# A fused DFT and SwiGLU kernel: three value units per tile seeded by ScalarE, one mirrored value kept in its bank, one row moved to another queue

## The chip, the cores and the metric

The kernel runs on one core of a Trainium2 chip. A core has five engines with their own instruction streams: TensorE (PE in the profile, with its weight loads as PEld), VectorE (DVE), ScalarE (ACT), GpSimd (POOL) and SyncE (SP). Each works through its stream in the order in which the program emits it, and they wait for each other through semaphores. Matrix products land in PSUM, which has eight banks here in use as three for gate values (g), three for values (v) and two for outputs (o).

The metric is the device time of one execution in microseconds. The median of three runs of the kernel before is 638.0 us (635.74 to 638.57).

## The reference

The input x has the shape (8, 3008, 256). It is transformed by a Fourier transform along both the sequence and the feature axis, and the real part of the result, as 24064 rows of 256, goes through a gated feed-forward block with 1536 inner features.

```python
X = np.fft.fft(x, axis=1); X = np.fft.fft(X, axis=2); x = X.real      # (24064, 256)
g = x @ w_gate
silu = g * (1.0 / (1.0 + np.exp(-g)))
val = x @ w_val
out = silu * val @ w_out
```

## The kernel before

The real part of a two-dimensional transform is symmetric: row k and row -k of a batch are a sum and a difference of the same two parts, an even part P and an odd part Q. So the kernel computes P and Q for half of the rows (12032 columns) and gets two output rows from each column. The columns are cut into 24 tiles: four widths of 512 and two of 480 in the first six (tiles 0 and 3 are 480 wide), then 512, and 320 plus 8 single columns in the last.

The feature transform is folded into the weights. Wp and Wq are the cosine and sine transforms of w_gate and w_val, and Wm is Wq times -2, with its first row (the one of frequency 0 and 128, which has its own sign) set to 0. So the direct value of a column is Wp P + Wq Q, and the mirrored value is the direct one plus Wm Q.

The main loop (line 954) runs over 288 **units** u = (t, f): tile t, and block f of 128 inner features, twelve per tile. For each unit `part_a` makes the direct gate and value, and `part_b`, one unit later, the mirrored ones. The products feed an output product with Wo (`OWork`, line 722), whose eight matmuls per unit are spread over the units of the next tile, and whose results ScalarE evicts to EV (line 709) before SP stores them.

There are two forms of unit.

- A **whole** unit has six matmuls: g gets Wp P and Wq Q, v gets Wp P and Wq Q, then after the direct values are read, Wm Q is added to g and to v. ScalarE takes Silu of g twice (L809 and L827), and DVE multiplies twice (L810 into hp, L828 into hm).
- A **split** unit has five. DVE forms es, the part of the value that the mirrored row shares, from the bank after Wp P alone and the first row of Q: es = bc * w0 + e (L795). `bc` is that row of Q copied to all partitions, and w0 the first row of the sine-transformed w_val. After Wq Q is added (in `odd`, emitted one unit later), DVE makes hp (L799), and the mirrored value as 2 es - e into an SBUF tile VV, in reversed order (L801). ScalarE writes Silu of the mirrored gate reversed (sgv, L823), and POOL, which works on SBUF alone, multiplies the two into hm (L824).

`WHOLE` (line 761) lists the whole units: all of tile 0, units 0 and 6 of tile 1, 2 and 9 of tile 2, 2 and 10 of tile 3, unit 10 of every later tile, and 10 and 11 of the last. That makes 39 whole units and 249 split ones.

The banks rotate (`Banks`, line 82): a unit takes the bank that has been unused longest, so that with three value banks unit f takes that of unit f-3. A transform (`transform`, line 594) takes one out of turn (aside).

Within one turn of the loop for unit i the order on each engine is the order of emission. First come the row steps and other work due before it, then `part_a(i)`: on PE g from Wp and Wq, then the value's Wp; on ScalarE sg; on DVE es. Then four output matmuls; then `odd` of unit i-1: on PE the value's Wq, on DVE hp and the mirrored value; then `part_b(i-1)`: on PE Wm into the gate, on ScalarE the mirrored Silu, and the product. Then an eviction, if one is due, four more output matmuls, folding steps on POOL, and a transform if one is due. Transforms are emitted after units 4 and 6 of tiles 2, 3, 5, 6, 7, 9, 10, 12, 13, 15, 16, 18, 19 and 21. They come in two parts: part 0 for the transforms of tiles 2, 5, 7, 10, 13, 16 and 19, part 1 for the others.

The row bc of tile t+1 goes by way of DRAM: `store_row0` (L944) ahead of unit 7 of tile t, `load_row0` (L949) ahead of unit 9, both by SP's queue, where the loads of x and the stores of the output stand too.

Of the kernel before, what the change touches and what calls it, by code (L numbers as in the profile page):

```python
# [12 lines left out]
F32 = mybir.dt.float32  # L13
I32 = mybir.dt.int32
BF16 = mybir.dt.bfloat16
AF = mybir.ActivationFunctionType
Alu = mybir.AluOpType
# [14 lines left out]
def kernel(  # L32
# [8 lines left out]
    nc = tc.nc  # L41
    B, M, D = x.shape
    Dff = moe_w_gate.shape[1]
    P = 128
# [4 lines left out]
    nF = Dff // P  # L49
    T = 512  # L50
# [6 lines left out]
    nT = len(wide)  # L57
# [4 lines left out]
    NOO = NCE + GH + 1  # L62
    NTAB = NOO + G
# [3 lines left out]
    def width(t):  # L67
        return wide[t]
# [5 lines left out]
    const = ctx.enter_context(tc.tile_pool(name="const", bufs=1))  # L74
# [7 lines left out]
    class Banks:  # L82
# [2 lines left out]

        def __init__(self, nm):
            self.line = [psB.tile([P, T], F32, name=f"{nm}{i}") for i in range(3)]

        def tile(self, shape=None, dt=None, name=None, aside=False):
            b = self.line.pop(0)  # L90
            self.line.insert(1 if aside else 2, b)
            return b if shape is None or len(shape) == 2 else b.rearrange("p (q d) -> p q d", q=shape[1])

    psG, psV = Banks("g"), Banks("v")

    Wp = const.tile([P, 2, Dff], BF16, name="Wp")
    Wq = const.tile([P, 2, Dff], BF16, name="Wq")
    Wm = const.tile([P, 2, Dff], BF16, name="Wm")
# [4 lines left out]
    w0 = const.tile([P, nF], F32, name="w0")  # L103
# [4 lines left out]
    mM = const.tile([P, 4], F32, name="mM")  # L108
    wC = const.tile([P, 1], F32, name="wC")
    sgn = const.tile([P, 1], F32, name="sgn")  # L110
    XA = const.tile([P, 8, 2, D], F32, name="XA")
    XC = const.tile([P, 8, 2, D], F32, name="XC")
    CEs = {(nm, i): const.tile([P, 2, 2, 3 * P + 1], BF16, name=f"CE{nm}{i}") for nm in "ac" for i in range(2)}
# [6 lines left out]
    VV = const.tile([P, 4, T], F32, name="VV")  # L120
# [7 lines left out]
    def next_of(big, what):  # L128
        turn[what] += 1
        return big[:, (turn[what] - 1) % 4]  # L130
# [138 lines left out]
    for hi in range(2):  # L269
        q.dma_start(out=XC3[64 * hi:64 * hi + NCR, 0:2, :],  # L270
                    in_=rows_at(0, 2 * (P + 1) - 1 + 2 * hi * R, [[2 * D, NCR], [R * D, 2], [1, 2 * D]]))
    for hi in range(2):
        for a in range(2):
            q.dma_start(out=XC3[64 * hi:64 * hi + NCR, 2 + a, :],
                        in_=down_set(0, 3 - 2 * hi - a, JC, LC, NC_))
    q.dma_start(out=XC0[NCR:64 + NCR + 1:64, 0:2, 1],
                in_=rows_at(0, 0, [[2 * R * D, 2], [R * D, 2], [1, D]]))
# [79 lines left out]
    def weigh(lo, hi):  # L357
        vts(Tab[:, 1, 1, :, lo:hi], Tab[:, 1, 1, :, lo:hi], scalar1=wC, scalar2=None, op0=Alu.mult)
# [120 lines left out]
    def value_rows(fcs):  # L479

        n = T // P
        ps = psO.tile([P, T], F32, name="o")
        for fc in fcs:
            src = W0[1] if fc == 0 else Wraw[1][:, :, (fc - 1) * T:fc * T]
            for f in range(n):
                for no in range(2):
                    nc.tensor.matmul(ps[:, fc * n + f:fc * n + f + 1], src[:, no, f * P:(f + 1) * P],
                                     SDt[:, no, 0:1], start=(no == 0), stop=(no == 1))
        nc.scalar.copy(w0[:, fcs[0] * n:(fcs[-1] + 1) * n], ps[:, fcs[0] * n:(fcs[-1] + 1) * n])
# [73 lines left out]
    def pq_tiles(t):  # L563
        if t not in ptile:
            w = width(t) + B if t == nT - 1 else T
            ptile[t] = (pqp if t < nT - 1 else const).tile([P, w], BF16, name="Pt")
            qtile[t] = (pqp if t < nT - 1 else const).tile([P, w], BF16, name="Qt")
        return ptile[t], qtile[t]
# [186 lines left out]
    units = [(t, f) for t in range(nT) for f in range(nF)]  # L755
# [2 lines left out]
    owork = None  # L758

    ROW0 = (7, 9)  # L760
    WHOLE = {0: range(nF), 1: (0, 6), 2: (2, 9), 3: (2, 10), nT - 1: (10, 11)}

    bc = {}

    def split(u):

        return u[1] not in WHOLE.get(u[0], (10,))

    def part_a(u):
        t, f = u  # L770
        n = width(t)
        w = n + (B if t == nT - 1 else 0)
        fs = slice(f * P, (f + 1) * P)
        if f == 0:
            hts[t] = (hp.tile([P, nF, T + B], BF16, name="hp"), hp.tile([P, nF, T], BF16, name="hm"))
        Pt, Qt = pq_tiles(t)

        def mm(ps, Wt, gv, src, start, stop):
            nc.tensor.matmul(ps[:, :w], Wt[:, gv, fs], src[:, :w], start=start, stop=stop,  # L779
                             skip_group_check=True)  # L780

        g = psG.tile([P, T], F32, name="g")
        mm(g, Wp, 0, Pt, True, False)
        if u == (0, 0):
            v = psV.tile([P, T], F32, name="v")
            mm(v, Wp, 1, Pt, True, False)
        mm(g, Wq, 0, Qt, False, True)
        if split(u):
            e = psV.tile([P, T], F32, name="v")
            mm(e, Wp, 1, Pt, True, False)  # L790
            sg = sgp.tile([P, T], F32, name="sg")
            nc.scalar.activation(sg[:, :w], g[:, :w], AF.Silu)  # L792
            stt = nc.vector.scalar_tensor_tensor
            es = esp.tile([P, T], F32, name="es")
            stt(es[:, :n], bc[t][:, :n], w0[:, f:f + 1], e[:, :n], op0=Alu.mult, op1=Alu.add)  # L795

            def odd():
                mm(e, Wq, 1, Qt, False, True)
                nc.vector.tensor_tensor(hts[t][0][:, f, :w], sg[:, :w], e[:, :w], op=Alu.mult)  # L799
                vm = next_of(VV, "vv")  # L800
                stt(vm[:, n - 1::-1], es[:, :n], 2.0, e[:, :n], op0=Alu.mult, op1=Alu.subtract)  # L801
                state[u] = (g, vm)
            return odd
        if u != (0, 0):
            v = psV.tile([P, T], F32, name="v")
            mm(v, Wp, 1, Pt, True, False)
        mm(v, Wq, 1, Qt, False, True)
        sg = sgp.tile([P, T], F32, name="sg")
        nc.scalar.activation(sg[:, :w], g[:, :w], AF.Silu)  # L809
        nc.vector.tensor_tensor(hts[t][0][:, f, :w], sg[:, :w], v[:, :w], op=Alu.mult)  # L810
        state[u] = (g, v)

    def part_b(u):
        t, f = u
        w = width(t)
        Pt, Qt = pq_tiles(t)
        g, v = state.pop(u)
        for gv, ps in ((0, g), (1, v))[:1 if split(u) else 2]:
            nc.tensor.matmul(ps[:, :w], Wm[:, gv, f * P:(f + 1) * P], Qt[:, :w], start=False, stop=True,  # L819
                             skip_group_check=True)  # L820
        if split(u):
            sg = sgv.tile([P, T], F32, name="sgv")
            nc.scalar.activation(sg[:, w - 1::-1], g[:, :w], AF.Silu)  # L823
            nc.gpsimd.tensor_tensor(hts[t][1][:, f, :w], sg[:, :w], v[:, :w], op=Alu.mult)  # L824
            return
        sg = sgp.tile([P, T], F32, name="sg")
        nc.scalar.activation(sg[:, :w], g[:, :w], AF.Silu)  # L827
        nc.vector.tensor_tensor(hts[t][1][:, f, w - 1::-1], sg[:, :w], v[:, :w], op=Alu.mult)  # L828
# [12 lines left out]
    for b in range(2, B, 2):  # L841
        u = slot[(b, 0)] - 1
# [64 lines left out]
    job_at = {}  # L907
    for jb in jobs[1:]:
        u = slot[jb]
# [13 lines left out]
    def sine_o(ch):  # L923
# [2 lines left out]
    late = angles_o(1)  # L926
    before = {0: late[0:1], 1: weight_unit(1, 0) + late[1:2], 2: weight_unit(1, 1) + cosine_o(0), 3: late[2:3],
              4: weight_unit(2, 0), 5: weight_unit(2, 1) + cosine_o(1), 7: sine_o(0), 8: sine_o(1),
              9: [lambda: weigh(NOO, NTAB), lambda: value_rows((1, 2))]}
    loads = []  # L930

    def spread_row0(t):
# [5 lines left out]

    row0d = {}

    def store_row0(t):
        w = width(t) + (B if t == nT - 1 else 0)
        row0d[t] = rdp.tile([1, T], BF16, name="row0")
        nc.sync.dma_start(out=row0d[t][:, :w], in_=pq_tiles(t)[1][0:1, :w])  # L944

    def load_row0(t):
        w = width(t) + (B if t == nT - 1 else 0)
        bc[t] = bcp.tile([P, T], BF16, name="bc")
        nc.sync.dma_start(out=bc[t][:, :w], in_=row0d.pop(t)[0, :w].partition_broadcast(P))  # L949

    prev = None
    odd = None
# [1 line left out]
    for i, u in enumerate(units):  # L954
        t, f = u
        if (t, f) == (1, 0):
            spread_row0(t)
        if 0 < t < nT - 1 and f in ROW0:
            (store_row0, load_row0)[ROW0.index(f)](t + 1)
        for fn in before.pop(i, ()):  # L960
            fn()
        run_loads(i)
        coming = part_a(u)
        if owork:
            owork.run(4)
        if odd:
            odd()
        odd = coming
        if prev is not None:
            part_b(prev)  # L970
            run_evicts()
            if prev[1] == nF - 1:
                owork = OWork(prev[0], hts[prev[0]])
                owork.run(4)
        if owork and not (prev is not None and prev[1] == nF - 1):
            owork.run(4)
        for what, j in fold_at.get(i, ()):
            fold_step(what, j, i)
        for what in act_at.pop(i, ()):
            load_next(what)  # L980
        if i in job_at:
            transform(*job_at[i])
        prev = u
# [38 lines left out]
```

## Time and profile before

| What | Value |
|---|---|
| median of 3 runs | 638.0 us |
| profiled execution, whole time | 638.3 us |
| its span, first to last instruction | 636.5 us |
| mean granted TensorE clock | 0.997 |
| DVE es (L795), 128x512 | 229 of 746 ns |
| DVE mirrored value (L801), 128x512 | 229 of 681 ns |
| POOL product (L824), 128x512 | 229 of 1278 ns |
| ScalarE Silu (L792), 128x512 | 229 of 602 ns |
| ScalarE eviction (L709), 128x512 | 90 of 580 ns |

A line of the profile's page of groups gives the source line, the engine and operation, what it writes and reads, the shape and count, then the busy time in us, the mean of one in ns, and the idle time ahead of it with what ended it. A line of the timeline gives the start in us from the beginning of the span, the duration in us, the engine, the source line, the operation and its tiles, and in brackets the idle time of the engine ahead of it with its releaser. PE's matmuls are pipelined: one of 512 columns has a duration of 0.38 us there, but the next starts 0.22 us later, and the chain of waits counts it so. A line of a table of windows gives the stretch, its length, then the busy time of PE, PEld, DVE, ACT and POOL with their counts, the granted clock of PE, the share of the DMA engines and their rate.

### The profile page before, as it was taken

The page shows a single profiled execution, that of the slowest core. Times are in us where ns is not written, and L with a number is a line of the kernel's source. Part 1 is how long each engine was busy: PE and PEld are TensorE (multiplying, and loading weights), DVE is VectorE, ACT ScalarE, POOL GpSimd, SP SyncE. Part 2 cuts the span into 40 slices and gives each one's busy share as a digit, 9 for nine tenths or more (in the row PEclk, how much of TensorE's full clock was granted, in tenths as well). Part 3 has the DMA queues.
Part 4 walks back from the last instruction along what each step waited for, and adds up shares of the span by engine and source line. Part 5 has one row for each costly group of instructions (what it writes and reads, how often), then busy time and mean ns, then how long its engine had stood idle before and what let it go on. Part 6 is the DMA issues. An engine that isn't in the chain of part 4 may idle for free.

```text
span 636.5 us, 13211 instructions
## 1 busy us (share of the span) xinstructions
PE 620.9 (98%) x4166; PEld 400.8 (63%) x4232; DVE 580.3 (91%) x1040; ACT 414.8 (65%) x744; POOL 516.9 (81%) x534
## 2 busy tenths in 40 slices
PE   8999998999999999999999999999999999999997
PEld 5446665666666666666666666656666666666686
DVE  7889996999999999999999999999999999999992
ACT  7686664666666666666666666666666666666663
POOL 9997998799699999996997988997798655655651
PEclk9999998999999999999999999999999999999999
DMA  9683224425322513245224511134211111111212
GB/s 228 117 170 82 82 83 147 126 74 147 100 70 79 165 44 86 66 93 147 76 78 105 131 43 52 45 84 140 58 47 47 42 51 44 58 46 46 57 50 76
DMA packets 52980, 55.41 MB, mean 87 GB/s; under 512 B 7504, under 2 KB 44238, under 8 KB 52910
## 3 DMA queue, kind: packets, MB, share of 16 engines
q1 hardware_dynamic: 49726, 52.20, 29.2%
q0 software_dynamic: 3184, 2.36, 2.5%
q8 instruction: 33, 0.54, 0.4%
q14 instruction: 37, 0.30, 0.2%
HBM read 32.22 MB, written 24.67 MB: 89 GB/s over the span
## 4 chain that ended last, share of the span: by engine, by line
PE 80%; DVE 11%; issue 2%; ACT 1%; DMA 1%; SPq 0%; POOL 0%; DVEq 0%; ACTq 0%
PE o L749 34%; PE v L779 19%; PE g L779 15%; PE g L819 8%; DVE hp L799 4%; DVE VV L801 2%; DVE Pt L639 2%; PE v L607 2%; DVE es L795 2%; PE v L819 1%; PE g L607 1%; DMA bc<-row 1%; PE o L466 0%; ACT sg L809 0%; DVE hp L810 0%
## 5 line engine op out<-in xcount | busy, mean ns | idle before, releaser
L824 POOL TENSOR_TENSOR hm<-sgv,VV 128x512 bf16<-128x512 f32 (+2 forms) x249 | 312.2, 1259 | 98.6 <-DVE VV L801 77.9
L823 ACT ACTIVATE sgv<-g 128x512 f32<-128x512 f32 (+2 forms) x249 | 146.9, 590 | 130.9 <-PE g L819 125.6
L795 DVE SCALAR_TENSOR_TENSOR es<-bc,w,v 128x512 f32<-128x512 bf16 (+2 forms) x249 | 183.4, 736 | 23.0 <-DMA bc<-row 4.3
L792 ACT ACTIVATE sg<-g 128x512 f32<-128x512 f32 (+2 forms) x249 | 148.0, 594 | 46.8 <-PE g L779 33.4
L749 PE MATMUL o<-Wo,hp 128*128 128x256 bf16 (+2 forms) x1140 | 170.5, 273 | 0.0
L749 PE MATMUL o<-Wo,hm 128*128 128x256 bf16 (+2 forms) x1140 | 169.6, 273 | 0.0
L799 DVE TENSOR_TENSOR hp<-sg,v 128x512 bf16<-128x512 f32 (+2 forms) x249 | 167.4, 672 | 0.3 <-PE v L779 0.2
L801 DVE SCALAR_TENSOR_TENSOR VV<-es,v 128x512 f32<-128x512 f32 (+2 forms) x249 | 167.3, 672 | 0.0
L749 PEld LDWEIGHTS <-hp 128*128 128x128 bf16 (+2 forms) x1140 | 112.5, 99 | 70.9 <-issue 2.4
L749 PEld LDWEIGHTS <-hm 128*128 128x128 bf16 (+2 forms) x1140 | 111.9, 98 | 71.4 <-issue 3.5
L779 PE MATMUL v<-Pt,Wp 128*128 128x512 bf16 (+2 forms) x288 | 108.1, 375 | 5.3 <-DVE VV L801 2.3
L779 PE MATMUL v<-Qt,Wq 128*128 128x512 bf16 (+2 forms) x288 | 108.2, 376 | 2.8 <-DVE es L795 2.8
L819 PE MATMUL g<-Qt,Wm 128*128 128x512 bf16 (+2 forms) x288 | 108.1, 375 | 0.7 <-ACT sg L809 0.7
L779 PE MATMUL g<-Pt,Wp 128*128 128x512 bf16 (+2 forms) x288 | 108.4, 377 | 0.1
L779 PE MATMUL g<-Qt,Wq 128*128 128x512 bf16 (+2 forms) x224 | 83.9, 375 | 0.3 <-DVE Qt L639 0.3
L779 PEld LDWEIGHTS <-Wp 128*128 128x128 bf16 x576 | 56.3, 98 | 43.8 <-issue 7.4
L779 PEld LDWEIGHTS <-Wq 128*128 128x128 bf16 x576 | 56.5, 98 | 12.0 <-issue 1.2
L709 ACT COPY EV<-o 128x512 f32<-128x512 f32 x90 | 52.2, 580 | 4.8 <-PE o L749 4.8
L819 PEld LDWEIGHTS <-Wm 128*128 128x128 bf16 x327 | 32.0, 98 | 9.8 <-issue 4.1
L188 POOL TENSOR_TENSOR SDf<-XA 128x1020 f32<-128x1020 f32 x14 | 33.0, 2356 | 3.4 <-DMA XC<-in_x_dram 3.4
L828 DVE TENSOR_TENSOR hm<-sg,v 128x512 bf16<-128x512 f32 (+2 forms) x39 | 25.9, 663 | 6.0 <-ACT sg L827 5.5
L810 DVE TENSOR_TENSOR hp<-sg,v 128x512 bf16<-128x512 f32 (+2 forms) x39 | 25.8, 660 | 5.3 <-ACT sg L809 4.9
(170 smaller groups left out, 480.2 us busy)
## 6 DMA issues: line engine op xcount, KB each, us to landing
out_dram<-EV SPq DMA_DIRECT2D x96, 128.0 KB
XA<-in_x_dram SPq DMA_DIRECT2D x32, 256.0 KB
XA<-in_x_dram SPq DMA_DIRECT2D x112, 64.0 KB
XC<-in_x_dram SPq DMA_DIRECT2D x210, 16.0 KB
XC<-in_x_dram SPq DMA_DIRECT2D x56, 60.0 KB
bc<-row SPq DMA_DIRECT2D x20, 128.0 KB
out_dram<-EV SPq DMA_DIRECT2D x12, 120.0 KB
out_dram<-EV SPq DMA_DIRECT2D x10, 112.0 KB
```

Of the source, the lines that this page charges most:

```text
L188: tt(C[:, :, 1:D], up[:, :, 1:D], down[:, :, D - 1:0:-1], op=Alu.add)
L709: nc.scalar.copy(ev[:, 0:len(pair), :], ps[:, 0:len(pair), :])
L749: nc.tensor.matmul(ps[:n, j, :], hts[minus][:, f, c:c + n], Wo[:, f, :], start=(f == 0), stop=(f == nF - 1))
L779: nc.tensor.matmul(ps[:, :w], Wt[:, gv, fs], src[:, :w], start=start, stop=stop, skip_group_check=True)
L792: nc.scalar.activation(sg[:, :w], g[:, :w], AF.Silu)
L795: stt(es[:, :n], bc[t][:, :n], w0[:, f:f + 1], e[:, :n], op0=Alu.mult, op1=Alu.add)
L799: nc.vector.tensor_tensor(hts[t][0][:, f, :w], sg[:, :w], e[:, :w], op=Alu.mult)
L801: stt(vm[:, n - 1::-1], es[:, :n], 2.0, e[:, :n], op0=Alu.mult, op1=Alu.subtract)
L819: nc.tensor.matmul(ps[:, :w], Wm[:, gv, f * P:(f + 1) * P], Qt[:, :w], start=False, stop=True, skip_group_check=True)
L823: nc.scalar.activation(sg[:, w - 1::-1], g[:, :w], AF.Silu)
L824: nc.gpsimd.tensor_tensor(hts[t][1][:, f, :w], sg[:, :w], v[:, :w], op=Alu.mult)
L828: nc.vector.tensor_tensor(hts[t][1][:, f, w - 1::-1], sg[:, :w], v[:, :w], op=Alu.mult)
```

## The change

It has three parts.

- **More split units.** `WHOLE` keeps tile 0, unit 0 of tile 1 and units 10 and 11 of the last tile: 15 whole units, 273 split. For some split units (`ON_V`: 6 in tile 1, 2 and 9 in tiles 2 and 3, 7 in every other) the mirrored value is written back into the unit's own bank, in order and not reversed, and DVE multiplies it there (L828, with ScalarE's Silu in order as in a whole unit) instead of POOL. These are 25 units.
- **Seeded units.** For units 1, 3 and 10 of a tile, ScalarE writes bc * w0 into the bank (`seed`), after `part_a` of the unit before and ahead of everything else of that turn. The Wp matmul then adds to it rather than starting anew, and es is a copy of the bank by ScalarE instead of DVE's L795. So that the direct value is not counted twice, the odd part is added with Wz, which is -0.5 Wm (Wq with its first row 0). A bank is seeded only if matmuls have begun it over at least the unit's width since a transform last took it, and not in a turn with a transform.
- **One row.** The store and the load of tile 3's row are issued by ScalarE's queue; the others stay with SP.

```diff
@@ Banks
+            self.begun = {id(b): 0 for b in self.line}
...
+            if aside:
+                self.begun[id(b)] = 0
@@
+    SEED = (1, 3, 10)
+    Wz = const.tile([P, len(SEED), P], BF16, name="Wz")
@@
-    WHOLE = {0: range(nF), 1: (0, 6), 2: (2, 9), 3: (2, 10), nT - 1: (10, 11)}
+    WHOLE = {0: range(nF), 1: (0,), nT - 1: (10, 11)}
+    ON_V = {1: (6,), 2: (2, 9), 3: (2, 9)}
...
-        return u[1] not in WHOLE.get(u[0], (10,))
+        return u[1] not in WHOLE.get(u[0], ())
+    def on_v(u):
+        return u[1] in ON_V.get(u[0], (7,))
+    seeded = {}
+    def seed(u):
+        t, f = u
+        w = width(t) + (B if t == nT - 1 else 0)
+        if f in SEED and split(u) and psV.begun[id(psV.line[0])] >= w:
+            seeded[u] = e = psV.tile()
+            nc.scalar.activation(e[:, :w], bc[t][:, :w], AF.Copy, scale=w0[:, f:f + 1])
@@ part_a
-            e = psV.tile([P, T], F32, name="v")
-            mm(e, Wp, 1, Pt, True, False)
+            mine = u in seeded
+            e = seeded.pop(u) if mine else psV.tile()
+            mm(e, Wp, 1, Pt, not mine, False)
+            if not mine:
+                psV.begun[id(e)] = w
...
-            stt(es[:, :n], bc[t][:, :n], w0[:, f:f + 1], e[:, :n], op0=Alu.mult, op1=Alu.add)
+            if mine:
+                nc.scalar.copy(es[:, :n], e[:, :n])
+            else:
+                stt(es[:, :n], bc[t][:, :n], w0[:, f:f + 1], e[:, :n], op0=Alu.mult, op1=Alu.add)
             def odd():
-                mm(e, Wq, 1, Qt, False, True)
+                if mine:
+                    nc.tensor.matmul(e[:, :w], Wz[:, SEED.index(f), :], Qt[:, :w], start=False, stop=True,
+                                     skip_group_check=True)
+                else:
+                    mm(e, Wq, 1, Qt, False, True)
                 nc.vector.tensor_tensor(hts[t][0][:, f, :w], sg[:, :w], e[:, :w], op=Alu.mult)
-                vm = next_of(VV, "vv")
-                stt(vm[:, n - 1::-1], es[:, :n], 2.0, e[:, :n], op0=Alu.mult, op1=Alu.subtract)
+                if on_v(u):
+                    vm = e
+                    stt(e[:, :n], es[:, :n], 2.0, e[:, :n], op0=Alu.mult, op1=Alu.subtract)
+                else:
+                    vm = next_of(VV, "vv")
+                    stt(vm[:, n - 1::-1], es[:, :n], 2.0, e[:, :n], op0=Alu.mult, op1=Alu.subtract)
@@ part_b
-        if split(u):
+        if split(u) and not on_v(u):
@@ before
+              11: [lambda k=k, f=f: nc.scalar.activation(Wz[:, k, :], Wm[:, 1, f * P:(f + 1) * P], AF.Copy, scale=-0.5)
+                   for k, f in enumerate(SEED)]}
@@
+    def row_queue(t):
+        return nc.scalar if t == 3 else nc.sync
...
-        nc.sync.dma_start(out=row0d[t][:, :w], in_=pq_tiles(t)[1][0:1, :w])
+        row_queue(t).dma_start(out=row0d[t][:, :w], in_=pq_tiles(t)[1][0:1, :w])
...
-        nc.sync.dma_start(out=bc[t][:, :w], in_=row0d.pop(t)[0, :w].partition_broadcast(P))
+        row_queue(t).dma_start(out=bc[t][:, :w], in_=row0d.pop(t)[0, :w].partition_broadcast(P))
@@ main loop, after part_a(u)
+        if i not in job_at and i + 1 < len(units):
+            seed(units[i + 1])
```

More of the change, by code (lines that the diff above doesn't have):

```diff
@@ L806, in part_a @@
             mm(v, Wp, 1, Pt, True, False)
+        psV.begun[id(v)] = w
         mm(v, Wq, 1, Qt, False, True)
@@ L928 @@
               4: weight_unit(2, 0), 5: weight_unit(2, 1) + cosine_o(1), 7: sine_o(0), 8: sine_o(1),
-              9: [lambda: weigh(NOO, NTAB), lambda: value_rows((1, 2))]}
+              9: [lambda: weigh(NOO, NTAB), lambda: value_rows((1, 2))],
+              11: [lambda k=k, f=f: nc.scalar.activation(Wz[:, k, :], Wm[:, 1, f * P:(f + 1) * P], AF.Copy, scale=-0.5)
+                   for k, f in enumerate(SEED)]}
     loads = []
```

## The prediction

> **What bounds the kernel now.** I read, in this order: the engines' busy shares, the chain of waits, one window of 40 us from the middle, and then the timeline of a single unit.
>
> ```profile
> PE 620.9 (98%) x4166; PEld 400.8 (63%) x4232; DVE 580.3 (91%) x1040; ACT 414.8 (65%) x744; POOL 516.9 (81%) x534
> ...
> PE 80%; DVE 11%; issue 2%; ACT 1%; DMA 1%; SPq 0%; POOL 0%; DVEq 0%; ACTq 0%
> ```
> ```profile
> 240.00:280.00 40.00, 39.62 (x262) 25.20 (x266) 37.81 (x62) 26.04 (x46) 38.38 (x39) 1.00 0.27 76
> ```
>
> TensorE (PE) is busy 39.62 of 40 us at clock 1.00, with the largest share of the chain. So a matmul taken away is a gain, and a wait put in front of one is a loss of its full length. VectorE (DVE), 37.81 of 40, is nearly as full. ScalarE (ACT), at 26.04, has room, but its instructions run in order. Below, "e(f)" is the first matmul of unit f into its value bank (Wp by Pt). This is one unit of tile 11, from e(9) to e(10):
>
> ```profile
> 322.47 0.68 DVE L799 TENSOR_TENSOR hp<-sg,v 128x512 bf16<-128x512 f32 x1
> 322.58 0.38 PE L779 MATMUL v<-Pt,Wp 128*128 128x512 bf16 x1
> 322.79 0.60 ACT L792 ACTIVATE sg<-g 128x512 f32<-128x512 f32 x1 [0.21 <-PE g L779]
> 323.07 0.68 DVE L801 SCALAR_TENSOR_TENSOR VV<-es,v 128x512 f32<-128x512 f32 x1
> 323.24 0.38 PE L779 MATMUL v<-Qt,Wq 128*128 128x512 bf16 x1
> 323.86 0.75 DVE L795 SCALAR_TENSOR_TENSOR es<-bc,w,v 128x512 f32<-128x512 bf16 x1
> 323.93 0.60 ACT L823 ACTIVATE sgv<-g 128x512 f32<-128x512 f32 x1 [0.55 <-PE g L819]
> 324.52 0.68 DVE L799 TENSOR_TENSOR hp<-sg,v 128x512 bf16<-128x512 f32 x1
> 324.54 0.38 PE L779 MATMUL v<-Pt,Wp 128*128 128x512 bf16 x1
> ```
>
> PE's period is 324.54 - 322.58 = 1.96 us, DVE's 324.52 - 322.47 = 2.05 (0.60 from hp to VV, 0.79 from VV to es, 0.66 from es to hp). DVE falls back 0.09 us per split unit and catches up at whole units. The VV at 323.07 is unit 7's: it ends at 323.75 and frees the bank that e(10) takes at 324.54. That leaves 0.79 us of **slack**, the quantity that decides this change.
>
> **Matmuls removed.** Twenty-four units cease to be whole (1 in tile 1, 2 each in tiles 2 and 3, 1 each in tiles 4 to 22). Each loses the Wm matmul into the value bank, which in the chain of waits takes this long:
>
> ```profile
> 78.96 0.22 PE v L819
> ```
>
> 24 x 0.22 = **-5.2 us**, all on the bound engine.
>
> **Row of tile 3.** The one long wait on a row, and what it does to PE:
>
> ```profile
> DVE es L795 <- DMA bc<-row: 4.3, 1, 4.3
> ```
> ```profile
> 93.04 0.26 SPq L944 DMA_DIRECT2D row<-Qt  x1
> 98.90 0.36 SPq L949 DMA_DIRECT2D bc<-row  x1
> 102.58 0.71 DVE L795 SCALAR_TENSOR_TENSOR es<-bc,w,v 128x480 f32<-128x480 bf16 x1 [4.27 <-DMA bc<-row]
> ```
> ```profile
> 97.87 0.37 PE L779 MATMUL v<-Pt,Wp 128*128 128x480 bf16 x1
> ...
> 103.35 0.38 PE L779 MATMUL v<-Qt,Wq 128*128 128x480 bf16 x1 [2.76 <-DVE es L795]
> ...
> 104.78 0.61 PE L779 MATMUL g<-Pt,Wp 128*128 128x480 bf16 x1
> ...
> 108.36 0.37 PE L779 MATMUL v<-Pt,Wp 128*128 128x480 bf16 x1
> ...
> 110.24 0.37 PE L779 MATMUL v<-Pt,Wp 128*128 128x480 bf16 x1
> ```
>
> From e(0) to e(3) of tile 3 pass 108.36 - 97.87 = 10.49 us. Three undisturbed units, one of them whole, would take 3 x 1.88 (110.24 - 108.36) + 0.2 = 5.85. The stall costs **4.6 us**: 2.76 of waiting, the rest in matmuls of 0.61 instead of 0.37 us after it. ScalarE's queue takes the place of SP's:
>
> ```profile
> 87.82 0.61 DVE L639 TENSOR_TENSOR Qt<-g,od 128x188 bf16<-128x188 f32 x2
> 87.85 0.60 ACT L792 ACTIVATE sg<-g 128x512 f32<-128x512 f32 x1
> ...
> 91.70 0.68 DVE L799 TENSOR_TENSOR hp<-sg,v 128x512 bf16<-128x512 f32 x1
> ```
> ```profile
> SPq L949 <- DMA row<-Qt: 11.0, 10, 1.9
> ```
>
> The store now stands ahead of the sg at 87.85 and waits for the Qt pieces, to about 88.7 us; with 0.26 of issue that sg starts near 89.0. The hp that needs it is due at 91.70, so this is hidden (without that cover, 1.1 us). Behind it wait sgv and POOL's product, late by at most as much. The load stands two units later (87.85 + 2 x 1.96, about 91.8). SP never waited more than 1.9 us for the row, so it can be issued there; with the 3.7 us from issue to use (102.58 - 98.90) it is in by 95.5, ahead of 98.3 (102.58 - 4.27) when tile 3 first wants it. No other row shows a wait, so next in line is nothing on this path. Gain **-4.6**, bounds -4.6 and 0.
>
> **VectorE and POOL.** The 66 seeded es leave DVE (units 1, 3, 10 of 23 tiles, less the first of tiles 1 and 4, whose bank was begun only 480 wide, and unit 10 of the last). 24 es, 24 mirrored values and one hm come: DVE is relieved by 42 x 0.75 - 24 x 0.68 - 0.69 = 14 us in all, off the path by itself. POOL has 248 products instead of 249.
>
> **The seeds.** ScalarE gets 66 seeds and 66 copies: no more than 66 x (0.72 + 0.58) = 86 us on 415, so its total fits. The order matters. A seed for unit f stands behind sg(f-1), waits until the bank of unit f-3 is free, and e(f) waits for it.
>
> ```profile
> L472 ACT ACTIVATE Wm<-o,m 128x512 bf16<-128x512 f32 x2 | 1.4, 718 | 0.0
> ...
> L433 ACT ACTIVATE SBa<-SA 128x512 bf16<-128x512 f32 x2 | 1.1, 619 | 0.0
> ```
>
> No ScalarE write into a bank is shown. L472 too takes its scale from a column: 0.72 us. L433, with a constant scale, gives the lower bound of 0.62; L472's longer one of 0.74 the upper. I take 0.72 as the nearest form. The Trainium skill (ScalarE: Activation LUTs, What ACT_TABLE_LOAD costs) has a column operand add about 93 ns, which agrees with the two rows. Its tip in Step-by-step, that a ScalarE write to PSUM is quicker than one to SBUF, no row here shows; by it the seed would lie nearer 0.62 and the sum about 2 us lower.
>
> For units 1 and 3 the bank is free early (the DVE has just been relieved), sg(f-1) ends 1.15 us ahead of e(f) (323.39 against 324.54), and 0.72 with two hand-overs fits: no cost, 0.2 us in tile 3. **Unit 10** takes the bank of unit 7, and unit 7's value now stays in that bank until DVE's hm (L828) has read it. That hm follows vm directly and needs its result. Rows for one DVE instruction reading the one before, and for a bank passed from DVE to PE:
>
> ```profile
> L828 DVE TENSOR_TENSOR hm<-sg,v 128x512 bf16<-128x512 f32 x23 | 15.8, 689 | 3.9 <-ACT sg L827 3.4
> ```
> ```profile
> 19.03 1.13 DVE L532 SCALAR_TENSOR_TENSOR VV<-VV,mM 128x376 f32<-128x376 f32 x2
> 20.19 0.62 DVE L349 TENSOR_SCALAR SDf<-VV 128x752 int32<-128x752 int32 x1
> ```
> ```profile
> 294.31 0.68 DVE L801 SCALAR_TENSOR_TENSOR VV<-es,v 128x512 f32<-128x512 f32 x1
> 295.04 0.38 PE L779 MATMUL v<-Pt,Wp 128*128 128x512 bf16 x1 [0.25 <-DVE VV L801]
> ```
>
> hm ends 0.03 + 0.69 = 0.72 after vm. Add 0.05 to ScalarE, 0.72 for the seed, 0.05 to PE: e(10) comes 1.54 us after vm's end at the earliest. PE's delay is 1.54 less the slack. vm writing into its bank I price at VV's 0.68; es's 0.75 bounds it above. The slack in a tile with a transform at units 4 and 6, both kinds:
>
> ```profile
> 299.55 0.68 DVE L801 SCALAR_TENSOR_TENSOR VV<-es,v 128x512 f32<-128x512 f32 x1
> ...
> 300.89 0.38 PE L779 MATMUL v<-Pt,Wp 128*128 128x512 bf16 x1
> ```
> ```profile
> 273.49 0.68 DVE L801 SCALAR_TENSOR_TENSOR VV<-es,v 128x512 f32<-128x512 f32 x1
> ...
> 275.00 0.38 PE L779 MATMUL v<-Pt,Wp 128*128 128x512 bf16 x1
> ```
>
> 0.66 us in tile 10 (part 0), 0.83 in tile 9 (part 1). There the transforms set DVE's lateness afresh, so the seeds of units 1 and 3 do not help. In a tile without transforms they do:
>
> ```profile
> 312.82 0.38 PE L779 MATMUL v<-Pt,Wp 128*128 128x512 bf16 x1
> ...
> 313.62 0.75 DVE L795 SCALAR_TENSOR_TENSOR es<-bc,w,v 128x512 f32<-128x512 bf16 x1
> ```
>
> es(4) now starts 0.80 after e(4). With unit 3 seeded its floor is hp(2) at 1.04 after e(3) (323.62 - 322.58), then 0.60 and 0.79, less one period: 0.47, call it 0.5. The slack becomes 0.79 + 0.3 = 1.08. So PE loses 0.88 us in 6 tiles (5, 7, 10, 13, 16, 19), 0.71 in 6 (6, 9, 12, 15, 18, 21), 0.46 in 7 (4, 8, 11, 14, 17, 20, 22): 5.3 + 4.3 + 3.2 = **+12.8**. Bounds: 10.9 with 0.62 for the seed, 14.5 with 0.74 and a vm of 0.75. Behind the waiting seed stand sgv(8), an eviction and sg(10), each up to 1 us late. The gate bank of unit 8 is wanted only two periods later and POOL's product waits for DVE anyway, so none reaches PE.
>
> Tiles 1 to 3 keep values at other units: their unit 10 costs 0.46, 0.16 and 0.06 by the same sum, and the value kept at unit 2 of tile 2 delays e(5) by 0.5; with the 0.2 above, **+1.4** (0 to 2). Three small activations for Wz in tile 0: 0 to 0.6, I take **+0.2**.
>
> Sum: -5.2 - 4.6 + 12.8 + 1.4 + 0.2 = **+4.6 us** on the profiled execution's 638.3 (span 636.5 and 1.8 around it), 642.9. The median of the runs shown is 0.3 lower: **642.6 us**. Its own range, with the bounds, is 639 to 647.
>
> **Rivals.**
>
> 1. *The seed of unit 10 is hidden.* If vm(7) runs so early that hm and seed end before e(10), only the gains remain: 638.0 - 9.8 + 0.2 = 628.4. It decides from a slack of 1.54. For it: seeds 1 and 3 give DVE back 0.75 us each. Against it: the slack is 0.66 to 0.83, and the transforms reset it between those seeds and unit 7.
> 2. *A draw.* Seeds at 0.62 and the small terms at nothing: 10.9 - 9.8 = +1.1, so 639.1.
> 3. *The row is no earlier*, because ScalarE's queue stands at the load: the 4.6 us stay, 647.2. Against it: SP's waits of 1.9 us at most.
> 4. *The clock.* If each new wait cooled PE as the one at 103.35 did (4.6 - 2.76 = 1.8 us more), 19 x 1.8 = 34 us, 677. The waits here are under a third of that one, and the clock is 1.00 in the window above, where such short ones occur. The Trainium skill (TensorE: Matmul & The Clock Gate, What's actually happening) asks for an idle window of about 3.4 us, by which there would be none; the 2.76 us that sufficed here is shorter than that, so the row keeps the rival alive.
>
> **How the numbers follow.** A difference of 0.5%, 3.2 us, is about what a measurement of this kernel can tell from no change. Forecast 50%, hidden 22%, draw 20%, row 5%, clock 3%. Slower: nine tenths of the forecast, the row and the clock, 53%. Same: the draw and the forecast's low edge, 25%. Faster: 22%. The range 628 to 648 leaves out about half of the hidden case and the clock.
>
> **What would show it.** Right: PE's e matmul (v from Pt and Wp) waits for ScalarE's seed once per tile from tile 4 on, 0.4 to 0.9 us; the seed is 0.72 us and waits for hm; es in tile 3 waits for no row; 24 fewer v matmuls at the Wm line. Wrong: PE has no idle time ahead of e(10), or waits at units 1 and 3 too, or the row's wait is still there.

## The result and the profile after

The changed kernel takes 657.7 us in the median of six runs (655.65 to 661.55), the kernel before 636.83 (635.64 to 638.57) in six runs beside it: 1.0328 times as long, 95% interval 1.0294 to 1.0362. The forecast was 642.6 with a range of 628 to 648. The profiled execution of the changed kernel took 658.1 us, its span is 656.2. Below are its busy shares and its chain of waits.

```profile
span 656.2 us, 13281 instructions
...
PE 621.4 (95%) x4142; PEld 399.6 (61%) x4208; DVE 569.8 (87%) x1023; ACT 475.0 (72%) x879; POOL 515.2 (79%) x533
...
PE 48%; DVE 17%; ACT 6%; issue 4%; DVEq 0%; ACTq 0%
```

The parts went where the diff sends them: PE has 24 matmuls fewer (4166 to 4142), DVE lost 10.5 us, ScalarE gained 60.2. But PE's busy time did not fall with the matmuls, its share fell from 98 to 95%, and the chain now runs through DVE and ScalarE for 23% of the span. So PE waits, and some of its matmuls got slower. The place is found by the times at which tiles begin: the first matmul of unit 0 of tiles 3, 4, 5, 6 and 23 in the timeline of PE, first of the changed kernel, then of the one before (tile 3's there, 97.87, stands in the prediction).

```profile
98.49 0.37 PE L800 MATMUL v<-Pt,Wp 128*128 128x480 bf16 x1
...
133.32 0.38 PE L800 MATMUL v<-Pt,Wp 128*128 128x512 bf16 x1
...
161.38 0.38 PE L800 MATMUL v<-Pt,Wp 128*128 128x512 bf16 x1
...
187.77 0.38 PE L800 MATMUL v<-Pt,Wp 128*128 128x512 bf16 x1
...
624.65 0.30 PE L800 MATMUL v<-Pt,Wp 128*128 128x328 bf16 x1
```
```profile
127.96 0.38 PE L779 MATMUL v<-Pt,Wp 128*128 128x512 bf16 x1
...
151.58 0.38 PE L779 MATMUL v<-Pt,Wp 128*128 128x512 bf16 x1
...
177.41 0.38 PE L779 MATMUL v<-Pt,Wp 128*128 128x512 bf16 x1
...
605.12 0.30 PE L779 MATMUL v<-Pt,Wp 128*128 128x328 bf16 x1
```

Tile 3 lasts 34.83 us (133.32 - 98.49) where it lasted 30.09, tile 4 28.06 where it lasted 23.62: +4.7 and +4.4. From tile 5 to the start of tile 23 the change is +9.7 (463.27 against 453.54), 18 tiles of 0.4 to 0.8 each. Two separate losses, then: one at a single place, where the forecast had its gain of 4.6, and one in every tile.

**The loss at tile 3.** The waits of the SP engine's DMA queue, its timeline and that of ScalarE's queue in the changed kernel:

```profile
SPq L166 <- DMA row<-Qt: 11.2, 1, 11.2
```
```profile
78.34 1.07 SPq L720 DMA_DIRECT2D out_dram<-EV  x3
90.60 0.27 SPq L166 DMA_DIRECT2D XC<-in_x_dram  x1
```
```profile
89.48 0.47 ACTq L986 DMA_DIRECT2D row<-Qt  x1
...
91.88 0.35 ACTq L991 DMA_DIRECT2D bc<-row  x1
```

SP issues nothing from 79.4 (78.34 + 1.07) to 90.60. What it waits for at line 166 is the store of the row, which ScalarE issued at 89.48, where it was due. Yet line 166 loads x into XC and touches no row. The kernel before, at this place, went on loading:

```profile
80.00 0.32 SPq L161 DMA_DIRECT2D XC<-in_x_dram  x1
80.36 3.54 SPq L164 DMA_DIRECT2D XC<-in_x_dram  x4
```

The link is in the list of the program's instructions and the semaphores that each waits for. A DMAHW semaphore counts finished transfers. This program has eight, DMAHW0 to DMAHW7, shared by SP's and ScalarE's queues and dealt out in turn; each transfer is held at its issue until the earlier transfer of its semaphore is done. The first number in a row counts the engine's instructions.

```
SP       129 L166 XC<-in_x_dram   waits DMAHW3
SP       130 L166 XC<-in_x_dram   waits DMAHW5
SP       131 L166 XC<-in_x_dram   waits DMAHW7
...
SP       136 L166 XC<-in_x_dram   waits DMAHW4
ScalarE  122 L986 row<-Qt         waits DMAHW4, DVE
ScalarE  127 L991 bc<-row         waits DMAHW6, DMAHW4
```

The row's store was dealt semaphore 4 between SP's instructions 129 and 130, and its load 6 between 130 and 131. When the number 4 comes round, SP's load 136 has to wait until the row's store is done, and the store waits for Qt. A little later SP is held once more, for 3.0 us at line 169, by the row's load. SP's instructions run far ahead of the tile they are for, ScalarE's do not, so an early load of x is tied to a late store. What the missing loads do to the other engines, in the grouped waits (us in total, times, longest):

```profile
POOL SDf L193 <- DMA XC<-in_x_dram: 15.1, 2, 12.7
...
ACT sgv L859 <- POOL hm L860: 8.7, 2, 8.2
...
PE g L800 <- ACT sgv L859: 7.0, 1, 7.0
DVE VV L836 <- POOL hm L860: 6.7, 1, 6.7
...
DVE es L822 <- DMA bc<-row: 3.1, 1, 3.1
```

and in the timeline of all engines:

```profile
98.59 0.20 POOL L214 TENSOR_TENSOR BBc<-EOf 128x2 bf16<-128x2 f32 x1
...
111.46 2.34 POOL L193 TENSOR_TENSOR SDf<-XC 128x1020 f32<-128x1020 f32 x1 [12.67 <-DMA XC<-in_x_dram]
...
115.21 0.57 ACT L859 ACTIVATE sgv<-g 128x480 f32<-128x480 f32 x1 [8.18 <-POOL hm L860]
...
115.83 0.56 PE L800 MATMUL g<-Pt,Wp 128*128 128x480 bf16 x1 [6.98 <-ACT sgv L859]
116.19 0.60 PE L800 MATMUL g<-Qt,Wq 128*128 128x480 bf16 x1
```

POOL stands 12.67 us for the load. Its products hm stand behind it; ScalarE's sgv waits for the sgv buffer that POOL has not read; PE waits 6.98 us for the gate bank that sgv has not read. Then the clock: matmuls take 0.60 us, and the granted clock is 0.50 from 116 to 120 us. Two windows of the changed kernel (PE, PEld, DVE, ACT, POOL busy, then the granted clock and DMA's share and GB/s):

```profile
80.00:120.00 40.00, 32.31 (x214) 20.34 (x215) 30.53 (x59) 22.34 (x43) 26.99 (x29) 0.89 0.27 67
...
240.00:280.00 40.00, 39.34 (x260) 25.25 (x262) 35.66 (x58) 30.99 (x57) 38.92 (x40) 1.00 0.21 63
```

PE lost 7 us there, and the transfers moved 67 GB/s. Tile 4 pays a second time: its own row came 3.1 us late (the es line above), SP being behind, and the granted clock falls again (0.83 in the mean from 135 to 145 us).

**The loss in every tile.** The end of tile 10 in the changed kernel, vm into the bank (L833), mirrored product (L864), seed (L788), e(10):

```profile
312.12 0.69 DVE L833 SCALAR_TENSOR_TENSOR v<-es,v 128x512 f32<-128x512 f32 x1
...
312.92 0.69 DVE L864 TENSOR_TENSOR hm<-sg,v 128x512 bf16<-128x512 f32 x1
...
313.12 0.38 PE L800 MATMUL g<-Qt,Wq 128*128 128x512 bf16 x1
...
313.64 0.69 ACT L788 ACTIVATE v<-bc,w 128x512 f32<-128x512 bf16 x1 [1.41 <-DVE hm L864]
...
314.38 0.38 PE L800 MATMUL v<-Pt,Wp 128*128 128x512 bf16 x1 [0.89 <-ACT v L788]
```

This is the chain of the forecast, link by link: PE stands for the seed of unit 10, which stood for hm, which stood for vm. The bracket gives PE 0.89 us of idle time, counted from the end of the matmul at 313.12. But the next matmul would have started 0.22 us after that one's start, not 0.38, so e(10) comes 314.38 - 313.34 = 1.04 us late.

### The profile page after: what moved, and what is told of

Read it like the earlier page. It is cut to its first block, busy times and chain, and to the rows that moved or that the text cites. A ratio compares the mean times of both kernels' runs of the same rounds, so it can differ in the third digit from the quotient of the medians.

```text
span 656.2 us, 13281 instructions
## 1 busy us (share of the span) xinstructions
PE 621.4 (95%) x4142; PEld 399.6 (61%) x4208; DVE 569.8 (87%) x1023; ACT 475.0 (72%) x879; POOL 515.2 (79%) x533
## 4 chain that ended last, share of the span: by engine, by line
PE 48%; DVE 17%; ACT 6%; issue 4%; DVEq 0%; ACTq 0%
PE o L754 20%; PE v L800 9%; PE g L800 7%; DVE hp L830 5%; PE g L855 5%; DVE VV L836 3%; ACT v L788 3%; DVE es L822 2%; DVE Qt L644 2%; PE v L612 2%; DVE hm L864 2%; DVE v L833 2%; ACT sgv L859 2%; ACT sg L816 2%; PE g L612 1%
## 5 line engine op out<-in xcount | busy, mean ns | idle before, releaser
L830 DVE TENSOR_TENSOR hp<-sg,v 128x512 bf16<-128x512 f32 (+2 forms) x273 | 183.8, 673 | 25.3 <-PE v L800 21.4
L816 ACT ACTIVATE sg<-g 128x512 f32<-128x512 f32 (+2 forms) x273 | 163.2, 598 | 42.6 <-PE g L800 31.4
L822 DVE SCALAR_TENSOR_TENSOR es<-bc,w,v 128x512 f32<-128x512 bf16 (+2 forms) x207 | 152.4, 736 | 21.2 <-DMA bc<-row 3.1
L800 PE MATMUL v<-Qt,Wq 128*128 128x512 bf16 (+2 forms) x222 | 83.5, 376 | 2.2 <-DVE es L822 2.2
L788 ACT ACTIVATE v<-bc,w 128x512 f32<-128x512 bf16 (+2 forms) x66 | 45.1, 683 | 23.9 <-DVE hm L864 21.4
L800 PEld LDWEIGHTS <-Wq 128*128 128x128 bf16 x510 | 50.0, 98 | 15.7 <-issue 7.9
L820 ACT COPY es<-v 128x512 f32<-128x512 f32 (+2 forms) x66 | 38.6, 586 | 0.0
L855 PEld LDWEIGHTS <-Wm 128*128 128x128 bf16 x303 | 29.7, 98 | 9.1 <-issue 3.5
```

Of the source, the lines that this page charges most:

```text
L788: nc.scalar.activation(e[:, :w], bc[t][:, :w], AF.Copy, scale=w0[:, f:f + 1])
L820: nc.scalar.copy(es[:, :n], e[:, :n])
```

## The experiments

Two theories were tested. **A**: the loss at tiles 3 and 4 is the row's transfers on ScalarE's queue, through SP's held loads. **S**: the loss in every tile is the seed of unit 10 behind the kept value of unit 7. Each kernel was timed beside the kernel before on the same chip; the two medians stand as this / before, then the ratio with its 95% interval. Tile lengths are compared with the profile of before as above. None of these kernels leaves out a part of the computation.

**1. The changed kernel, the row back on SP's queue.**

```
-        return nc.scalar if t == 3 else nc.sync
+        return nc.sync
```

> The changed kernel with tile 3's row back on SP's queue. Theory A (the row on ScalarE's queue holds SP's loads, because SP's later loads wait for the row's store, and this costs the 9.2 us by which tiles 3 and 4 became longer): SP's wait of 11.2 us for the row and POOL's wait of 12.7 us for a load are gone, tiles 3 and 4 together are within 1.5 us of the kernel before (with its old wait of 4.3 us for the row back), and the time is 636.8 + 10.5 to 11.5, so 647 to 648. Rival B (tiles 3 and 4 lose it through the values kept in the bank at units 2 and 9 and the seeds there): still 655 to 658.

Measured: 646.14 / 636.58, 1.0139 [1.0116, 1.0161]. Its waits:

```profile
PE v L800 <- ACT v L788: 13.5, 21, 2.0
...
POOL SDf L193 <- DMA XC<-in_x_dram: 3.0, 1, 3.0
...
DVE es L822 <- DMA bc<-row: 2.1, 1, 2.1
```

The time is a little below the expected, and tiles 3 and 4 together are 2.3 us shorter than in the profile of before, not within 1.5. SP's wait is gone, and so is POOL's of 12.7: the 3.0 is an earlier one, at 51 us, which the profile of before has too (3.4). The 2.0 of PE is at tile 3, where the seed of unit 1 now waits for the row. Tiles 3 and 4 now change by -2.8 and +0.5 instead of +4.7 and +4.4, tiles 5 to 22 by 0.4 to 0.8 as before. So the row's queue costs 657.7 - 646.1 = **11.6 us**, all of it at those two tiles, and everything else in the change costs 646.14 - 636.58 = **9.6 us**.

**2. The kernel before, tile 3's row on ScalarE's queue and nothing else.**

```
-        nc.sync.dma_start(out=row0d[t]...
+        (nc.scalar if t == 3 else nc.sync).dma_start(out=row0d[t]...
-        nc.sync.dma_start(out=bc[t]...
+        (nc.scalar if t == 3 else nc.sync).dma_start(out=bc[t]...
```

> The kernel before with only the row of tile 3 moved to ScalarE's queue. Theory A: SP waits about 11 us for the row's store, POOL then waits for a load of x, and the kernel becomes slower by 8 to 10 us: 645 to 647. Rival (the row alone does what was forecast, the wait of 4.3 us goes): 632. Rival B: no loss here, 632 to 637.

Measured: 647.12 / 636.58, 1.0158 [1.0125, 1.0191]. Its waits, of SP's queue and of all engines:

```profile
SPq L715 <- DMA row<-Qt: 10.9, 1, 10.9
```
```profile
POOL SDf L188 <- DMA XA<-in_x_dram: 13.6, 2, 12.8
...
PE g L779 <- ACT sgv L823: 7.0, 1, 7.0
```

With no seed in the kernel the same jam appears: SP held 10.9 us (here at a store of outputs), POOL 12.8, PE 7.0. Tile 3 is 5.0 longer, tile 4 6.3, all others from 5 on 0.0. Tile 2, in which ScalarE's queue issues both transfers, is unchanged (0.0), so ScalarE's own wait for Qt costs nothing, as forecast. Theory A holds by itself, at +10.5 in the median, a little more than the 8 to 10 expected.

**3. Unit 9 seeded instead of unit 10 (row on SP).** Experiment 1's edit and

```
-    SEED = (1, 3, 10)
+    SEED = (1, 3, 9)
```

> The changed kernel with the row on SP's queue and unit 9 seeded in place of unit 10, so that no seed takes the bank of unit 7. Theory S (only the seed behind the product of unit 7 costs PE time; the slack of unit 9's bank, 1.0 to 1.2 us, covers a seed of 0.7): PE waits for no seed from tile 4 on, each tile is 0.1 to 0.2 us shorter than before, and the time is 632 to 634. Rival (66 seeds and copies on ScalarE cost PE time wherever they stand): 645 to 648, as with unit 10.

Measured: 637.27 / 636.58, 1.0011 [0.9982, 1.0039]: neither number. The loss of 9.6 is gone (0.7 left), which speaks for S. But the gain that S left over did not appear. With the seed at unit 9, the unit 10 loses its 0.22 (its period falls from 2.17 to 1.95 us in tiles 9 to 11), and other units give it back: the period from e(0) to e(1) is 2.03 to 2.13 instead of 1.95. There the seed of unit 1 waits for the bank of unit 10 of the tile before. The VV that frees it did not exist while that unit was whole, and DVE comes to it late (experiment 9 shows when):

```profile
ACT v L788 <- DVE VV L836: 16.9, 36, 0.8
```

So tiles 4 to 22 change by -0.1 to +0.1 us, apart from tiles 10 and 14 with +0.3 and +0.2. Tile 3 ran slower than in experiment 1 by 1.3 us, with its row waiting 3.4.

**4. The changed kernel, the row on POOL's queue.**

```
-        return nc.scalar if t == 3 else nc.sync
+        return nc.gpsimd if t == 3 else nc.sync
```

> The changed kernel with tile 3's row on POOL's queue, whose transfers have completion semaphores of their own. Theory A (it is the completion semaphore shared by SP's and ScalarE's transfers that holds SP): SP does not wait, the row is there in time, and the time is 642 to 645, below the row on SP's queue by up to 4.6 us. Rival (any row off SP's queue holds the loads of x back): 655 to 658. If POOL reaches the load late: 645 to 650.

Measured: 645.29 / 636.58, 1.0127 [1.0104, 1.0150], a little above the 642 to 645 expected and just within what was expected if POOL reached the load late. SP is not held; tile 3 is 4.2 shorter than in the profile of before, and its row is waited for less than on SP:

```profile
ACT v L788 <- DMA bc<-row: 1.2, 1, 1.2
...
DVE es L822 <- DMA bc<-row: 0.8, 1, 0.8
```

In the list of this program POOL's transfers have semaphores of their own. Leaving SP's queue is not what hurts; sharing semaphores with it is. Against experiment 1 the earlier row is worth only 0.9 us.

**5. The kernel before, tile 3's row without any transfer**, spread over the partitions by a matmul and a ScalarE copy, as tile 1's row is (`t != 2` leaves out the transfers of the next tile's row, tile 3's):

```
-            if (t, f) == (1, 0):
+            if (t, f) in ((1, 0), (3, 0)):
                 spread_row0(t)
...
-            if 0 < t < nT - 1 and f in ROW0:
+            if 0 < t < nT - 1 and t != 2 and f in ROW0:
```

> The kernel before with tile 3's row copied to all partitions by one matmul and one ScalarE copy, as tile 1's is, and no transfer for it. It measures what the wait of 4.3 us on that row is worth alone. If the forecast's term was right (4.6 us): 631.5 to 633. If something stands right behind it (POOL's load of x, which came 1.2 us late in the same stretch): 633 to 635.

Measured: 634.61 / 635.70, 0.9981 [0.9972, 0.9990]. Tile 3 is 4.6 us shorter than in the profile of before, exactly the forecast's term; yet the median gains 1.1. The profile of before was an execution in which the stall cost more than usual, as experiments 8 and 10 show.

**6. Units 2, 4 and 9 seeded, row on POOL's queue.**

```
-    SEED = (1, 3, 10)
+    SEED = (2, 4, 9)
```

> The changed kernel with units 2, 4 and 9 seeded and tile 3's row on POOL's queue. Theory S: no seed waits for a late bank, so each tile from 4 on keeps most of the 0.22 us of the matmul it lost (19 tiles, 3 to 4 us), and tiles 3 and 4 are 4 us shorter: 628 to 631. Rival (66 seeds on ScalarE cost about what the matmuls give): 632 to 634.

Measured: 635.89 / 635.70, 0.9999 [0.9989, 1.0009]; both expectations missed. Moved one unit on, the first seed still waits for a bank: in tiles 10 and 11 the period from e(1) to e(2) is 2.22 and 2.23 us instead of 1.96. Tiles 4 to 22 change by -0.13 to +0.17.

**7. The value kept at unit 8 instead of 7 (row on SP, seeds at 1, 3, 10).**

```
-        return u[1] in ON_V.get(u[0], (7,))
+        return u[1] in ON_V.get(u[0], (8,))
```

> The changed kernel with the row on SP's queue, units 1, 3 and 10 seeded as in the change, but the value of unit 8 instead of unit 7 kept in its bank. Theory S (a seed costs PE time through the bank whose product is late, not by standing at unit 10): unit 10 now takes the bank of unit 7, free 0.7 us earlier, so its seed waits 0 to 0.2 us instead of 0.5 to 0.9; unit 11, not seeded, takes the late bank with 0.8 us to spare. Time 635 to 639. Rival (unit 10 is the wrong place for a seed): 645 to 647.

Measured: 636.89 / 635.70, 1.0042 [1.0019, 1.0065]. Against the kernel before beside it that is +1.2 where experiment 1 had +9.6; from tile 4's start to tile 23's it is -0.1 us against the profile of before, where experiment 1 has +10.4. One unit's shift is worth 8.4 to 10.5 us. In tile 10:

```profile
298.24 0.69 ACT L788 ACTIVATE v<-bc,w 128x512 f32<-128x512 bf16 x1 [0.62 <-DVE VV L836]
...
298.99 0.38 PE L800 MATMUL v<-Pt,Wp 128*128 128x512 bf16 x1
...
300.38 0.69 DVE L864 TENSOR_TENSOR hm<-sg,v 128x512 bf16<-128x512 f32 x1
...
301.12 0.38 PE L800 MATMUL v<-Pt,Wp 128*128 128x512 bf16 x1 [0.24 <-DVE hm L864]
```

The seed of unit 10 waits for an ordinary VV and e(10) for nothing; the kept bank goes to e(11), where there is no seed between hm and PE, and costs 0.24 (it was expected to have 0.8 us to spare). S is shown: the loss takes the kept value together with the seed behind it on one bank; without that seed a kept value costs about what the removed matmul gives.

**8. The kernel before, tile 12's row alone on ScalarE's queue**: experiment 2's edit with `t == 12`.

> The kernel before with only tile 12's row on ScalarE's queue. Theory A says that SP is held there too, but that the price depends on how far the loads of x are ahead: in tile 11 POOL wants them later. SP waits for the row by 1 to 10 us and the time is 636 to 640. Rival (a row on ScalarE's queue costs about 10 us wherever it stands, through ScalarE's own wait): 645 to 648.

Measured: 638.44 / 635.70, 1.0046 [1.0032, 1.0060]. Its waits, of SP's queue and of DVE in tile 13:

```profile
SPq L164 <- DMA row<-Qt: 8.3, 1, 8.3
```
```profile
355.51 0.75 DVE L795 SCALAR_TENSOR_TENSOR es<-bc,w,v 128x512 f32<-128x512 bf16 x1 [3.28 <-DMA bc<-row]
```

SP is held again, 8.3 us, but here the loads that it holds are not yet wanted; what comes late is tile 13's row, and of the tiles from 4 on 13 alone is longer, by 3.1 us. SP is held in the same way, and the price depends on what stands behind it.

**9. A version built from these**: the changed kernel with the other rows on SP, tile 3's row by matmul (experiment 5), the value kept at unit 8 in tiles 4 to 17 and 23, none kept in 18 to 22.

```
-        return u[1] in ON_V.get(u[0], (7,))
+        return u[1] in ON_V.get(u[0], (8,) if u[0] < 18 or u[0] == nT - 1 else ())
```

> A version put together from what was found: the changed kernel with tile 3's row copied by a matmul (no transfer), the value of unit 8 instead of unit 7 kept in its bank in tiles 4 to 17 and none in tiles 18 to 22, where POOL has room. Theory S: no late bank stands behind a seed, each tile costs what it did before or 0.1 us less, and the row is worth the 1.1 us that it was in the kernel before: 633 to 635. Rival (seeds, copies and the twelfth split unit cost as much as the matmuls give, wherever they stand): 634.5 to 637, no better than the kernel before with the copied row.

Measured: 633.46 / 636.51, 0.9958 [0.9942, 0.9973]: 3.05 us less than the kernel before. Its page:

```profile
span 631.4 us, 13291 instructions
...
PE 615.4 (97%) x4143; PEld 398.5 (63%) x4209; DVE 565.3 (90%) x1018; ACT 476.1 (75%) x880; POOL 521.7 (83%) x538
```

Where no value is kept, neither in the tile nor in the one before (19 to 22), a tile is 0.20 to 0.22 us shorter: the whole of the removed matmul, with three units seeded. So the seeds as such cost nothing. Where one is kept, in tiles 5 to 17, the tile changes by -0.15 to +0.08. Tile 18 keeps none but follows a tile that does, and is 0.12 shorter. The period from e(0) to e(1) is 2.03 us in tiles 5 to 18 and 1.95 in 19 to 22. So DVE is late for the seed of unit 1 where the tile before kept a value and DVE had its hm to do.

**10. The kernel before, unchanged, once more.**

> The kernel before, unchanged, for a second profile of it. The wait for tile 3's row was 4.3 us in the execution that the forecast read, whose time of 638.3 us is among the longest of this kernel, and 2.1 to 3.4 us in the profiles of kernels that leave that row with SP. If the wait differs from one execution to another, this profile shows 1 to 3.5 us and a time of 635 to 637; if 4.3 us is its usual size, 4 to 4.5 us again.

Measured: 637.42 / 636.51, 1.0006 [0.9990, 1.0023]. The wait for the row in tile 3 is there again at 4.2 us, not shorter as expected. What differs is what follows it:

```profile
103.33 0.36 PE L779 MATMUL v<-Qt,Wq 128*128 128x480 bf16 x1 [2.65 <-DVE es L795]
...
104.17 0.37 PE L779 MATMUL g<-Pt,Wp 128*128 128x480 bf16 x1
```

After 2.65 us of idle PE the matmuls ran at 0.37 us; after 2.76, in the first profile, at 0.61. The granted clock from 104.5 to 106 us is 1.00 here and was 0.50 there. Tile 3 is 1.8 us shorter for it, so of the 4.6 us only 2.8 came in this execution. In the profile of experiment 8, whose edit does not touch tile 3, the row is waited for 2.8 us and tile 3 is 3.2 us shorter than in the first profile: there the stall costs 1.4. The forecast had taken one execution's stall, cooled clock and all, for the kernel's.

## Why the prediction was wrong

The sign held, slower, and the reason given for it is real: it makes 9.6 of some 21 us. The larger part, and nearly all of the error, came from one step.

1. **"Row of tile 3", "Gain -4.6, bounds -4.6 and 0": this step failed.** Measured on either side of it, the move costs +11.6 (experiment 1) or +10.5 (experiment 2). The step worked out ScalarE's queue with care: the store at 89.48 and the load at 91.88 came within 0.9 us of its times. SP's queue it looked at only for whether the row waits there, and concluded "next in line is nothing on this path". Its bound of 0 supposed that taking two transfers away from SP can only free it. What holds SP is no wait that the diff adds in the text: the semaphores are dealt out over both queues, and the profile of before, where one queue uses them in order, cannot show the effect. What could have been read was that SP issues loads far ahead, and that those loads had nothing to spare: POOL waits 1.15 us for one at 99.38, in the very stretch. A tie between a queue that runs ahead and one that does not should have left a bound above zero. All the signs under "Right" came true in the changed kernel; none of them looked at SP.
2. **The rival "The row is no earlier" (647.2)** looked at the right edit with the wrong mechanism: it let the row stay as late as before because ScalarE's queue stands. In the changed kernel tile 3 waits for no row; the transfers that come late are SP's loads, and no rival had those.
3. **The other terms: +9.2 forecast (-5.2 + 12.8 + 1.4 + 0.2; 24 x 0.22 is 5.3), +9.6 measured.** The mechanism was right by place too: part 0 tiles +0.56 to +0.60 (forecast 0.88 - 0.22 = 0.66; tile 10 with +0.83 stands out), part 1 tiles +0.53 to +0.55 (0.49), tiles without a transform +0.39 to +0.40 (0.24), with 0.74 in tile 14. The delay of e(10), which is the period from e(9) to e(10) less the 1.95 us of before, was 0.78 to 0.82 in the part 0 tiles (0.88), 0.75 in part 1 (0.71), 0.62 without a transform (0.46), and 1.05 (1.04 by the lines above) and 0.96 in tiles 10 and 14. The idle times in the brackets, 0.89, 0.58 and 0.45 in tiles 10, 12 and 8, are 0.16 less; that 0.89 looks like the forecast's 0.88 is chance. Over tiles 4 to 22 the delays sum to 14.2 us (12.8, bounds 10.9 to 14.5). That the totals agree within 0.4 is luck in part: in experiment 1 tiles 4 to 22 lost 10.4 us where these terms give 8.6, and tile 3, whose row was waited for 2.1 us and not 4.3, was 2.8 shorter than in the profile of before. Tiles 1 and 2 together changed by +0.26 us.
4. **The durations** behind them: the seed takes 688 ns (forecast 720, lower bound 620), vm into its bank 688 (680), and hm starts 0.11 us after vm ends (312.92 - 312.81), not 0.03. The chain is then 0.11 + 0.69 + 0.03 + 0.69 + 0.05 = 1.57 us against the forecast 1.54. Two errors cancelled. What differed in the delays is the slack: in tile 10 vm ends at 312.81 and e(10) was due at 313.34, 0.53 us later and not 0.66; without a transform the slack was 0.95 (1.57 - 0.62) and not 1.08. The groups of the changed kernel at 512 columns:

```profile
L788 ACT ACTIVATE v<-bc,w 128x512 f32<-128x512 bf16 x61 | 42.0, 688 | 22.9 <-DVE hm L864 21.4 <-DVE VV L836 1.4
...
L833 DVE SCALAR_TENSOR_TENSOR v<-es,v 128x512 f32<-128x512 f32 x22 | 15.1, 688 | 0.0
```

5. **Seeds 1 and 3 cost nothing**, as forecast, and the 24 matmuls are worth 0.22 each: experiment 9's tiles without a kept value show both. Experiments 3 and 6 add what the forecast did not ask: a seed early in a tile costs 0.1 to 0.3 us when the value kept in the tile before makes DVE late for the VV that frees its bank. In the changed kernel it does not (1.95 us from e(0) to e(1) in tiles 5 to 22).
6. **The size of the row's stall**, 4.6 us, was right for the profiled execution (experiment 5 takes just that off tile 3) and too large for the kernel: its removal is worth 1.1 us in the median. In three profiles with nothing edited at tile 3 the stall cost 4.6, 2.8 and 1.4 us (before, experiments 10 and 8). The first has 1.8 us of cooled clock in it, which not every execution has: of 60 runs of the kernel before that were timed with the experiments, 17 show a mean clock of 0.997, as that profile does, and took 637.5 us or more; the other 43 show 0.999 or 1.000 and took 635.0 to 637.2. Experiment 5's profile also has 0.9 us more in tile 13; experiment 10, with no edit, has 0.6 there, and why is not known.
7. **The rival of the clock** was wrong for the seeds' waits (clock 1.00 between 240 and 280 us), but the mechanism it names occurred at tile 3, after the wait of 6.98 us.

The books: the forecast's base of 638.0 lay 1.2 above the 636.8 measured beside the changed kernel, the row was off by +16.2 (11.6 + 4.6), the rest by +0.4. Together that is +15.4, and 657.7 - 642.6 is 15.1.

Left open: why tiles 10 and 14 stand out by 0.2 to 0.3 us. In both, DVE's hp of unit 2 starts 3.44 us after e(2), behind ScalarE's copy of es, where in tiles 8, 11 and 13 it starts at 3.09. They stand out in experiments 3 and 7 as well, where no seed stands behind a kept value, and not in experiment 9. What makes hp late there was not tried.

## What to carry to other kernels

When a transfer moves to another engine's queue, ask not only when it is issued there, but what the queue it leaves will wait for: if both queues draw completion semaphores from one small pool, a stream of prefetches that runs ahead is tied to the moved transfer's issue. Move late-issued transfers to a queue with semaphores of its own, or do without the transfer. And a bank that is kept longer should not be the one whose next user has a step to do before TensorE: one unit further on, the same kept value cost some 9 us less.

## What was not expected of the hardware

- An issue queue stood 11.2 us (10.9 and 8.3 in experiments 2 and 8) for a transfer of another engine's queue with which it shares no data. The Trainium skill (DMA: Bandwidth & Descriptors, Issuing engines are not separate DMA queues) says that issuing from several engines saves only the issue time on the sequencer, usually small. No run here measures that saving. Issued from the second queue, this row cost 11.6 us, through the wait of the first.
- ScalarE with a scale from a column takes 688 ns for 512 columns into a bank, where the same form into SBUF took 718 in the mean of two, 0.69 and 0.74 us (the row of line 472 in the prediction, which reads 32-bit input). The Trainium skill (ScalarE: Activation LUTs, Step-by-step) has the write to PSUM as the quicker. The means agree in sign, by 30 ns, but one of the two took as long as a write into a bank, and the types differ, so these rows do not decide it.
- An idle PE of 2.76 us was followed by matmuls of 0.61 us (granted clock 0.50) in one execution, one of 2.65 us by matmuls of 0.37 (1.00) in another. The difference, 1.8 us of run time at one place, is larger than what several of the edits were worth.
- DVE reading its own last result out of a bank starts 0.11 us after that result is done (tile 10), where in SBUF it started 0.03 after.
